# The seventh pair's transpose: by a DMA in its own unit, or by TensorE in the next

## The chip, the cores and the metric

The kernel runs on one core of one Trainium2 chip. The metric is the device time of one execution in microseconds (us), and of several runs the median. All times below are us, counted from the first instruction of the profiled execution, unless marked ns.

## What is computed

Softmax attention with an extra term in the denominator, over 8 batches of 12 heads (sequence 448, head dimension 64), and then a two-layer block with the Mish activation over all 3584 rows:

```python
scores = scale * np.matmul(q, k.transpose(0, 1, 3, 2))        # 8 x 12 x 448 x 448
m = np.max(scores, axis=-1, keepdims=True)
e = np.exp(scores - m)
attn = e / (np.sum(e, axis=-1, keepdims=True) + np.exp(-m) + 1e-09)
x = rows of matmul(attn, v)                                   # 3584 x 768
h = x @ w_in                                                  # 3584 x 2048
out = (h * np.tanh(softplus(h))) @ w_out                      # 3584 x 768, float32
```

## The kernel before

**Pairs, steps and units.** Two heads make a pair: 6 pairs a batch, 48 in all, counted from 0, so that the seventh is pair 6 (`HEAD`). A pair has 4 steps. A step is one or two score tiles (`scores`, TensorE, L264 to L281), their negated row maximum (`negm`, VectorE, L285), and one exponential per tile (`exps`, ScalarE, L298), which also gives the row sums and writes `en` (queries on partitions). Three PSUM tiles (`sc`) let TensorE run three steps ahead of ScalarE, and step n+3's scores wait until step n's exponentials have read their tile. The first six pairs run in a loop of their own. After that three pairs form a unit: units 2 to 15 have attention work, 12 steps each (numbered n = 0 to 11; "steps" below are these), and each unit ends in eight blocks of the first matmul with Mish (`mm1_mish`, L438 and L444). From unit 4 on, pieces of the second matmul (`mm2_part`, L485) are spread over the steps as well. The first matmul of a batch is spread over two units, one batch behind the attention: units 2 and 3 do that of pairs 0 to 5.

**Turning a pair.** The product with v (`av_pair`, L407) wants keys on partitions, so `en` must be transposed to `eT`. `normalise` does that with one DMA transpose on the SyncE (SP) queue (L370; 28 blocks of 128 x 128). `turn_on_pe` does it in four parts j: seven TensorE transposes into one PSUM bank (L381) and one copy to `eT` (L385), mostly on VectorE. Which pairs go which way is in `BY_PE`: pair 5 is turned on TensorE in steps 1 to 4 of unit 2, pair 6 in unit 3 (two parts at step 0, two at steps 2 and 3), pair 7 in steps 4 to 7 of unit 3. Pair 8 goes by DMA, issued at the end of unit 2. `eT` has three buffers; a new pair's transpose waits until the buffer's last reader, an `av_pair`, is done.

**Dividing.** Pairs 0 to 11 are divided after the product with v: `spread_rden` (L341, 16 small matmuls) spreads the reciprocals (in two bf16 parts `hl`, written by GpSimd at L322 and L323) over a PSUM bank, a copy brings it to SBUF as `rb` (L350), and the product's evacuation multiplies by it (`xT`, L419, VectorE). In unit 2 the copy of `rb` is on ScalarE, in units 3 and 4 on VectorE. `RDEN_AT` and `AV_AT` list at which step a pair's spread and product stand: in unit 3 at steps 7, 9, 10 and 8, 10, 11 for pairs 6, 7, 8.

**What sets the order.** There is no scheduler: each engine runs its instructions in the order in which the code emits them. Evacuations are put on a list (`late`) and emitted at the next step, right after its exponentials (`flush_late`). Two PSUM banks (`mo`) go round among the turns, spreads, products and the blocks of both large matmuls; each user waits until the bank's last evacuation is done. SP issues, in order: loads of q, k, v (L125, three per pair, three pairs ahead or more), the DMA transposes, and output rows. The casts of loaded pairs (L166 to L168) and the loads of weight pieces (L152) are on GpSimd, in one order too; `W_AT` says at which step a piece is loaded.

The first lines to look at are these two from the unit loop, which tell that an evacuation follows the next step's exponentials on its engine:

```python
            exps(idx)
            flush_late()
```

Of the kernel before, what the change touches and what calls it, by code (L numbers as in the profile page):

```python
# [15 lines left out]
UNIT_PAIRS = 3  # L16
# [3 lines left out]
def kernel(  # L20
# [9 lines left out]
    nc = tc.nc  # L30
# [5 lines left out]
    NT = 4  # L36
# [5 lines left out]
    UNITS_PER_B = HP // UNIT_PAIRS  # L42
# [6 lines left out]
    STEPS = 4  # L49
# [46 lines left out]
    LATE_DIV = 2 * HP  # L96
# [230 lines left out]
    def spread_rden(p, copy=None):  # L327

        own = mo_take()
        r = own[:, :]  # L330
        hl = att[p]["hl"]
        half = SP_ * NT - 3 * 128
        for at in range(4):
            for x in range(2):
                for h in range(2):
                    if at < 3:
                        rows, c, q0 = slice(0, 128), at + 4 * h, 128 * at + half * h
                    else:
                        rows, c, q0 = slice(half * h, half * h + half), 3, 3 * 128 * (1 - h)
                    n = rows.stop - rows.start  # L340
                    nc.tensor.matmul(  # L341
                        r[h * D : (h + 1) * D, q0 : q0 + n],
                        lhsT=hl[rows, x, c : c + 1].to_broadcast([n, D]),
                        rhs=ident[rows, rows],
                        start=(x == 0), stop=(x == 1),
                    )

        def evac():
            rb[p] = rb_pool.tile([128, S], FP32, tag="rb", name="rb")
            (copy or nc.scalar.copy)(rb[p], r[:, 0:S])  # L350
            mo_free.append(own)

        if copy is None:
            spread_copy[p] = evac
        else:
            late.append(evac)
# [18 lines left out]
    def turn_on_pe(p, j, act=False):  # L375

        st = att[p]
        own = mo_take()
        ps = own[:, :].bitcast(BF16).rearrange("c (i q) -> c i q", q=128)
        for i in range(NTILE):  # L380
            nc.tensor.transpose(ps[0:SP_, i, :], st["en"][:, j, i, 0:SP_], ident)  # L381
        copy = nc.scalar.copy if act else nc.vector.tensor_copy

        def evac():
            copy(  # L385
                out=st["eT"][0:SP_, j, :].rearrange("c (i q) -> c i q", q=128),
                in_=ps[0:SP_, 0:NTILE, :],
            )
            mo_free.append(own)

        late.append(evac)
# [134 lines left out]
    LOAD_AT = (0, 3, 6)  # L526
    HEAD = HP

    BY_PE = {HEAD - 1: 1, HEAD: 0, HEAD + 1: STEPS}
    AV_AT = {0: {6: 3, 8: 4, 10: 5}, 1: {8: 6, 10: 7, 11: 8}}  # L530
    RDEN_AT = {0: {5: 3, 7: 4, 9: 5}, 1: {7: 6, 9: 7, 10: 8}, 2: {3: 10, 7: 11}}
    TURN_BY_ACT = {(HEAD - 1, 3)}

    W_AT = ({1: 1, 5: 1, 9: 1}, {1: 1, 5: 1, 7: 1, 9: 1, 11: 1}, {1: 1, 3: 1, 5: 1, 7: 1})
# [14 lines left out]
    for p in range(HEAD):  # L549
        for s in range(STEPS):  # L550
# [23 lines left out]
            if s == 3:  # L574
                if p >= 3:
                    av_pair(p - 3, hold=True)
                if p + 5 < 10:
                    load_pair(p + 5)
                normalise(p, dma=p not in BY_PE)
    denominators(HEAD - 1)  # L580
# [3 lines left out]
    for u in range(UNITS_PER_B, N_UNITS + 2 * UNITS_PER_B):  # L584
        attn = u < N_UNITS
        filler = deque()
        for part in plan.get(u, []):
            filler.extend(mm2_part(*part))
        total, done, acc = sum(w for _, w in filler), 0, 0.0
        p0 = u * UNIT_PAIRS  # L590
        if attn and u >= first_mm2:
            av_with.update({p0 + i: p0 + i - UNIT_PAIRS for i in range(UNIT_PAIRS)})
        end = min((u + 1) * UNIT_PAIRS, N_PAIRS) * STEPS

        for n in range(steps):
            pi, s = divmod(n, STEPS)
            p, idx = p0 + pi, p0 * STEPS + n
            late_tp = u == UNITS_PER_B and n == STEPS
            if late_tp:
                transpose_pair(p0 + 2)  # L600
            exps(idx)
            if late_tp:
                evac_qk(p0 + 2)
            if u == UNITS_PER_B + 1 and n == 0:
                for j in range(2):
                    turn_on_pe(HEAD, j)
            flush_late()
            acc += weight[n]
            want = int(total * acc / sum(weight) + 1e-6)
            while done < want:  # L610
                fn, w = filler.popleft()
                fn()
                done += w
            scores_ahead(end)
            if n in LOAD_AT:
                load_pair(p0 + LOAD_AT.index(n) + LEAD)
                cast_pair(p0 + LOAD_AT.index(n) + LEAD - 1)
            spread = RDEN_AT.get(u - UNITS_PER_B, {})
            if n in spread:
                spread_rden(spread[n], copy=None if u == UNITS_PER_B else nc.vector.tensor_copy)  # L620
            early = AV_AT.get(u - UNITS_PER_B)
            if early is not None:
                if n in early:
                    av_pair(early[n])
                for pe, n0 in BY_PE.items():
                    first = 2 if pe == HEAD else 0
                    if pe // UNIT_PAIRS == u - 1 and n0 + first <= n < n0 + NT:
                        turn_on_pe(pe, n - n0, act=(pe, n - n0) in TURN_BY_ACT)
            elif s == (2 if pi else 0) and N_PAIRS <= p < N_PAIRS + UNIT_PAIRS:
                av_pair(p - UNIT_PAIRS)  # L630
            if u - UNITS_PER_B < len(W_AT):
                load_w(W_AT[u - UNITS_PER_B].get(n, 0))
        assert done == total

        moe = u < N_UNITS + UNITS_PER_B
        b, w = (u - UNITS_PER_B) // UNITS_PER_B, u % UNITS_PER_B
        nxt = p0 + UNIT_PAIRS
        todo = sorted(range(p0, nxt), key=lambda p: p in BY_PE)
        for f in range(FF_U):
            if moe:  # L640
                mm1_mish(b, w * FF_U + f)
            if u == UNITS_PER_B and f in (2, 6) or u == UNITS_PER_B + 1 and f == 1:
                load_w(1)
            if not attn:
                continue
            if f == 0:
                denominators(p0, UNIT_PAIRS)
                for p in todo if p0 < LATE_DIV else todo[:1]:
                    normalise(p, dma=p not in BY_PE)
            if f == 5 and u == UNITS_PER_B + 1:  # L650
                spread_rden(p0, copy=nc.scalar.copy)
            if f == 4:
                scores_ahead(min(nxt * STEPS + 1, N_PAIRS * STEPS))
            if f in (1, 3, 5):
                transpose_pair(nxt + f // 2, bank=f // 2 % 2)
                evac_qk(nxt + f // 2)
            if f >= FF_U - 2:
                scores_ahead(min(nxt * STEPS + f - FF_U + 4, N_PAIRS * STEPS))
            if f in (3, FF_U - 1) and p0 >= LATE_DIV:
                p = todo[1 + f // (FF_U - 1)]  # L660
                normalise(p, dma=p not in BY_PE)
    flush_late()
# [31 lines left out]
```

## Time and profile before

| what | value |
|---|---|
| three runs, us | 489.28, 492.48, 492.93 |
| median, us | 492.48 |
| profiled execution, us | 488.69 |
| its span, first to last instruction, us | 486.9 |
| mean granted TensorE clock | 0.987 |
| instructions | 9223 |
| the first six pairs | 0 to 45 |
| unit 2: steps, then its eight blocks | 45.0 to 61.3, to 72.6 |
| unit 3: steps, then its eight blocks | 72.6 to 91.6, to 103.7 |
| unit 4: steps, then its eight blocks | 103.7 to 120.5, to 131.9 |
| a later unit (5): steps, then blocks | 131.9 to 146.9, to 158.5 |
| DMA transpose on SP, issue time, us | 4.0 least, 4.2 median, 9.6 most |
| DMA transpose, issue to landing, us | 6.1 least, 6.6 median, 11.7 most |

How to read it: the profiled execution took 488.69 us, of which 486.9 lie between its first and last instruction. "Busy" of TensorE includes waiting inside a pipelined matmul. The three executions that were timed lie within 3.65 us of each other. PE is TensorE, PEld its weight loads, DVE VectorE, ACT ScalarE, POOL GpSimd, SPq the SyncE queue. In the table by stage each engine has its busy time and, in brackets, its number of instructions, then the granted clock (1.00 is full), the share of time in which the core's 16 DMA engines were busy (a transfer that straddles the edge of a stage counts whole, so it can pass 1), and GB/s.

### The profile page before, as it was taken

To read this page: it belongs to the slowest core of one execution; us is meant where nothing else is said; L and a number is where in the kernel's file an instruction comes from. 1 tells how busy PE (TensorE), PEld (TensorE's weight loads), DVE (VectorE), ACT (ScalarE), POOL (GpSimd) and SP (SyncE) were. 2 spreads that over 40 slices of the span, in tenths; PEclk is the share of its full clock that TensorE was granted. 3 is DMA by queue.
4 is the path that set the end of the run, shared out by engine and by line. 5 is a ranking of instruction groups with operands and counts; after the bars stand their busy time and mean duration, and the time that the engine had idled before them with its cause. 6 is when DMAs were issued, how large, how long until landed. Compare 5 with 4: busy or idle time off the path is not lost.

```text
span 486.9 us, 9223 instructions
## 1 busy us (share of the span) xinstructions
PE 453.3 (93%) x3219; PEld 258.4 (53%) x3219; DVE 359.4 (74%) x713; ACT 345.4 (71%) x905; POOL 103.4 (21%) x184
## 2 busy tenths in 40 slices
PE   4676896898999999999999999999999999999996
PEld 2344454554655565555555555555555555556563
DVE  4889738758889898889899888889898978520011
ACT  5998859677687887879687868788797968412300
POOL 4534535206013030403012120404040200000000
PEclk9999798999999999999999999999999999999999
DMA  8999999999998979799999998998979886761122
GB/s 233 221 235 206 265 197 241 145 185 246 143 220 224 204 195 197 230 194 258 164 247 174 221 209 190 223 199 223 199 236 164 210 152 142 146 146 31 36 59 72
DMA packets 204975, 91.08 MB, mean 187 GB/s; under 512 B 161792, under 2 KB 201472, under 8 KB 204928
## 3 DMA queue, kind: packets, MB, share of 16 engines
q1 hardware_dynamic: 197440, 84.20, 79.5%
q0 software_dynamic: 7488, 6.29, 9.0%
q8 instruction: 25, 0.41, 0.4%
q14 instruction: 22, 0.18, 0.1%
HBM read 45.61 MB, written 11.01 MB: 116 GB/s over the span
## 4 chain that ended last, share of the span: by engine, by line
PE 75%; ACT 11%; DVE 8%; DMA 2%; issue 2%; SPq 1%; POOL 0%; DVEq 0%; ACTq 0%
PE mo L438 26%; PE mo L485 24%; ACT en L298 9%; PE sc L264 7%; DVE negm L285 6%; PE sc L407 5%; PE sc L438 4%; PE sc L186 3%; PE mo L407 2%; DMA k_f<-in_k_dram 1%; PE mo L341 1%; PE sc L270 1%; DMA v_f<-in_v_dram 1%; SPq L125 1%; DVE eT L385 1%
## 5 line engine op out<-in xcount | busy, mean ns | idle before, releaser
L298 ACT ACTIVATE en<-sc,negm 128x448 bf16<-128x448 f32 x336 | 208.4, 641 | 22.6 <-DVE negm L285 20.7
L285 DVE TENSOR_REDUCE negm<-sc 128x2 f32<-128x896 f32 x192 | 183.0, 971 | 44.8 <-PE sc L264 28.2
L485 PE MATMUL mo<-w_out_sb,gT 128*128 128x384 bf16 (+1 forms) x1024 | 166.7, 306 | 0.0
L438 PE MATMUL mo<-xT,w_in_sb 128*128 128x448 bf16 x672 | 141.9, 353 | 0.5 <-DVE xT L417 0.3
L485 PEld LDWEIGHTS <-gT 128*128 128x128 bf16 x1024 | 96.3, 98 | 55.4 <-issue 1.3
L444 ACT ACTIVATE gT<-mo 128x448 bf16<-128x448 f32 x112 | 59.6, 543 | 83.0 <-PE mo L438 82.7
L438 PEld LDWEIGHTS <-w_in_sb 128*128 128x128 bf16 x768 | 72.7, 98 | 63.6 <-issue 3.3
L166 POOL CAST q_bf<-q_f 112x512 bf16<-112x512 f32 x47 | 29.3, 623 | 230.8 <-DMA q_f<-in_q_dram 208.0
L362 DVE TENSOR_SCALAR en<-en,rden 128x448 bf16<-128x448 bf16 x252 | 73.6, 365 | 0.8
L264 PE MATMUL sc<-kT,qd 128*128 128x448 bf16 x252 | 71.6, 354 | 0.0
L298 ACT ACTIVATION_READ_ACCUMULATOR en<-sc,negm 128x1 f32 x336 | 71.1, 212 | 0.0
L472 DVE COPY o_sb<-mo 128x384 f32<-128x384 f32 (+1 forms) x64 | 32.1, 501 | 48.3 <-PE mo L485 48.1
L264 PEld LDWEIGHTS <-qd 128*128 128x128 bf16 x252 | 24.6, 97 | 28.8 <-issue 12.9
L407 PE MATMUL sc<-eT,v_bf 112*64 112x448 bf16 x288 | 34.1, 357 | 2.1 <-ACT en L298 1.6
L223 DVE TENSOR_SCALAR qd<-sc 64x448 bf16<-64x448 bf16 x72 | 27.7, 385 | 7.5 <-PE sc L186 6.6
L407 PEld LDWEIGHTS <-v_bf 112*64 112x64 bf16 x384 | 20.9, 111 | 22.3 <-issue 15.6
L168 POOL CAST v_bf<-v_f 112x512 bf16<-112x512 f32 x48 | 29.9, 624 | 12.2 <-DMA v_f<-in_v_dram 11.5
L167 POOL CAST k_bf<-k_f 112x512 bf16<-112x512 f32 x47 | 29.1, 619 | 9.1 <-DMA k_f<-in_k_dram 8.0
L270 PE MATMUL sc<-kT,qd 64*128 64x448 bf16 x36 | 15.8, 457 | 7.7 <-ACT en L298 7.2
L186 PEld LDWEIGHTS <-q_bf 112*128 112x128 bf16 x192 | 14.3, 103 | 15.4 <-DVE q_bf L166 4.2
L231 ACT COPY kT<-sc 128x448 bf16<-128x448 bf16 x39 | 20.8, 534 | 0.6 <-PE sc L186 0.6
L438 PE MATMUL sc<-xT,w_in_sb 128*128 128x448 bf16 x96 | 20.8, 353 | 0.0
(53 smaller groups left out, 279.2 us busy)
## 6 DMA issues: line engine op xcount, KB each, us to landing
q_f<-in_q_dram SPq DMA_DIRECT2D x48, 224.0 KB, 5.3
k_f<-in_k_dram SPq DMA_DIRECT2D x48, 224.0 KB, 5.4
v_f<-in_v_dram SPq DMA_DIRECT2D x48, 224.0 KB, 5.5
w_in_sb<-in_moe_w_in_dram POOLq DMA_DIRECT2D x12, 256.0 KB, 7.3
w_out_sb<-in_moe_w_out_dram POOLq DMA_DIRECT2D x8, 384.0 KB, 7.4
out_dram<-o_sb SPq DMA_DIRECT2D x7, 336.0 KB, 3.5
out_dram<-o_sb SPq DMA_DIRECT2D x8, 288.0 KB, 5.0
out_dram<-o_sb SPq DMA_DIRECT2D x8, 240.0 KB, 3.5
```

The source lines that it names most:

```text
L166: cast_q(out=q_bf, in_=q_f.rearrange(by_t, t=NT))
L167: cast_k(out=k_bf, in_=k_f.rearrange(by_t, t=NT))
L168: nc.gpsimd.tensor_copy(out=v_bf, in_=v_f)
L264: nc.tensor.matmul(sc[:, bk, 0:S], lhsT=qT[:, i].rearrange("d h r -> d (h r)"), rhs=kT, start=True, stop=True,)
L285: nc.vector.tensor_reduce(out=negm, in_=sc[:, 0 : len(cols), 0:S], axis=AX.X, op=ALU.max, negate=True)
L298: e = nc.scalar.activation(out=st["en"][:, :, c, 0:SP_], in_=sc[:, bk, 0:S].rearrange("q (j c) -> q j c", j=NT), func=AF.Exp, bias=st["neg ...
L362: nc.vector.tensor_scalar(out=en[:, :, i, 0:SP_], in0=en[:, :, i, 0:SP_], scalar1=st["rden"][:, i : i + 1], scalar2=None, op0=ALU.mult,)
L407: nc.tensor.matmul(av[h * 64 : (h + 1) * 64, 0:S], lhsT=v_bf[:, h, j * D : (j + 1) * D], rhs=e_h, start=(j == 0), stop=(j == NT - 1),)
L438: nc.tensor.matmul(h_ps[:, 0:S], lhsT=w_in_sb[:, dm, ff * 128 : (ff + 1) * 128], rhs=xT[b][:, dm, :], start=(dm == 0), stop=(dm == DM_T - 1),)
L444: nc.scalar.activation(out=gT[:, ff, b % 2 * S : b % 2 * S + S], in_=h_ps[:, 0:S], func=AF.Mish)
L472: nc.vector.tensor_copy(out=o_sb[:, cols], in_=st["o"][:, 0:n_cols])
L485: nc.tensor.matmul(st["o"][:, 0:n_cols], lhsT=gT[:, ff, i * 128 : (i + 1) * 128], rhs=w_out_sb[:, ff, cols], start=(ff == 0), stop=(ff == ...
```

## The change

Pair 6 leaves `BY_PE`. Its DMA transpose is issued in unit 2 at step 7, behind the product of pair 3 at step 6, from whose buffer of `eT` it takes over. Its 28 transposes, 28 weight loads and four copies in unit 3 are gone. In unit 3 the spread and product of pair 6 move from steps 7 and 8 to steps 0 and 1, the turn of pair 7 from steps 4 to 7 to steps 2 to 5, the product of pair 7 stays at step 8 and its spread moves from 9 to 7, and the spread and product of pair 8 move from 10 and 11 to 9 and 10. The five copies of `rb` at L350 in units 3 and 4 (pairs 6, 7, 8 and 10, 11) go from VectorE to ScalarE.

```diff
-    BY_PE = {HEAD - 1: 1, HEAD: 0, HEAD + 1: STEPS}
-    AV_AT = {0: {6: 3, 8: 4, 10: 5}, 1: {8: 6, 10: 7, 11: 8}}
-    RDEN_AT = {0: {5: 3, 7: 4, 9: 5}, 1: {7: 6, 9: 7, 10: 8}, 2: {3: 10, 7: 11}}
+    BY_PE = {HEAD - 1: 1, HEAD + 1: 2}
+    AV_AT = {0: {6: 3, 8: 4, 10: 5}, 1: {1: 6, 8: 7, 10: 8}}
+    RDEN_AT = {0: {5: 3, 7: 4, 9: 5}, 1: {0: 6, 7: 7, 9: 8}, 2: {3: 10, 7: 11}}
...
-            if u == UNITS_PER_B + 1 and n == 0:
-                for j in range(2):
-                    turn_on_pe(HEAD, j)
             flush_late()
...
             if n in spread:
-                spread_rden(spread[n], copy=None if u == UNITS_PER_B else nc.vector.tensor_copy)
+                spread_rden(spread[n], copy=None if u == UNITS_PER_B else nc.scalar.copy)
...
                 for pe, n0 in BY_PE.items():
-                    first = 2 if pe == HEAD else 0
-                    if pe // UNIT_PAIRS == u - 1 and n0 + first <= n < n0 + NT:
+                    if pe // UNIT_PAIRS == u - 1 and n0 <= n < n0 + NT:
                         turn_on_pe(pe, n - n0, act=(pe, n - n0) in TURN_BY_ACT)
...
+            if u == UNITS_PER_B and n == 7:
+                normalise(p0)
...
-                for p in todo if p0 < LATE_DIV else todo[:1]:
+                for p in [p for p in todo if p != HEAD] if p0 < LATE_DIV else todo[:1]:
                     normalise(p, dma=p not in BY_PE)
```

## The prediction

> **What bounds the kernel now.** I read the page first, then busy times by stage, then the chain of work that ended last in the stages that the change touches, then the timelines of PE, DVE, ACT and SP there.
>
> ```profile
> span 486.9 us, 9223 instructions
> PE 453.3 (93%) x3219; PEld 258.4 (53%) x3219; DVE 359.4 (74%) x713; ACT 345.4 (71%) x905; POOL 103.4 (21%) x184
> PEclk9999798999999999999999999999999999999999
> DMA  8999999999998979799999998998979886761122
> ```
>
> PE is busy 93%, but two slices, the fifth and the seventh, have a lower clock: units 2 and 3. DMA is busy nearly everywhere.
>
> ```profile
> core 0: us, PE busy (x) PEld busy (x) DVE busy (x) ACT busy (x) POOL busy (x), PEclk, DMA share, GB/s
> 61.30:72.60 11.30, 11.30 (x78) 5.89 (x77) 4.34 (x8) 6.35 (x12) 4.25 (x8) 1.00 1.20 193
> 72.60:91.60 19.00, 13.16 (x149) 8.99 (x148) 16.12 (x23) 16.77 (x46) 6.46 (x10) 0.91 1.01 199
> 103.70:120.50 16.80, 14.10 (x120) 8.01 (x119) 11.73 (x16) 14.38 (x42) 7.38 (x12) 1.00 1.15 245
> 131.90:146.90 15.00, 15.00 (x105) 8.47 (x103) 12.69 (x22) 13.64 (x39) 1.84 (x3) 1.00 0.98 227
> ```
>
> From 131.9 on PE has no idle time in this stage: whatever is saved before moves all that follows, and reaches the end. In unit 3's steps (72.6 to 91.6) PE is idle 5.8 of 19 us, and DVE and ACT are busy 16.1 and 16.8. The chain there:
>
> ```profile
> 80.29 1.08 DVE negm L285
> 81.37 0.19 DVE eT L385
> ...
> 88.61 0.61 DVE xT L419
> 89.27 0.70 PE mo L341 x16
> 89.97 1.67 PE mo L407 x16
> 91.64 2.38 PE mo L438 x12
> ```
>
> DVE alternates row maxima with copies of `eT`, and at the end PE does the last spread and two products after the last exponentials, before the unit's first block at 91.64. SP:
>
> ```profile
> 60.74 5.53 SPq L370 DMA_TRANSPOSE eT<-en  x1
> 66.36 0.55 SPq L125 DMA_DIRECT2D q_f<-in_q_dram  x1
> 88.64 18.91 SPq L370 DMA_TRANSPOSE eT<-en  x3
> 107.64 0.53 SPq L125 DMA_DIRECT2D q_f<-in_q_dram  x1
> ```
>
> Pair 8's transpose, loads of pairs 13 to 15 behind it, then transposes of 9 to 11 that begin when pair 6's product (ends 88.6) frees a buffer.
>
> **The change, part by part: unit 3.** Durations are starts to next starts in the timelines: a row maximum 1.00 (two tiles) or 0.53, a copy of `eT`, of `rb` on DVE, or an `xT` 0.53, an exponential 0.61, `rb` on ACT 0.43 (0.54 busy, next start 0.43 later at 58.33), a turn on PE 0.5, a spread 0.65, a product 0.88, two scores 0.3.
>
> Removed from DVE: four `eT` copies (2.1) and three `rb` copies (1.6), 3.7 of its 16.1. Removed from PE: 28 transposes with weight loads, four turns of 0.5, or 1.0 where the clock is half. Added to ACT: 3 x 0.43 = 1.3. ACT then has 21 x 0.61 + 1.3 = 14.1 from 74.43 on and could at best end at 88.5 (now 89.27, with 1.3 of waits for DVE). So the exponentials cannot gain much. What gains is the tail: now spread 8 and products 7 and 8 stand after the last step; afterwards product 8 stands at step 10.
>
> I follow the four engines through the new order with these durations. Exponentials 0 and 1 end at 75.66 and 76.88 as now; scores 3 start at 75.82, then spread 6, scores 4, ACT copies `rb` 6 at 77.3 and does step 2 from 77.75 to 78.97. DVE: maximum 4 to 78.85, `xT` 6 to 79.55, maximum 5 to 80.55, then `eT`, maximum 6 to 82.08, `eT`, maximum 7 to 83.13, `eT`, maximum 8 to 84.66, `eT`, maximum 9 to 86.2. ACT: step 8 from 84.75 to 86.0 (now 84.00 to 85.23: DVE's row up to here still has four copies, and `xT` 6 is new), `rb` 7 to 86.43, step 9 to 87.66, step 10 to 88.9, `rb` 8 to 89.33, step 11 to 89.94. PE: scores 11 at 86.05, product 7 to 87.3, spread 8 to 87.95, product 8 at 88.35 to 89.2; the unit's first block needs the bank that `rb` 8 frees at 89.33, so it starts at 89.4 instead of 91.6. Exponentials end 0.7 later, yet this is hidden: table load to 91.45, first Mish to 92.0, and the fourth block, the first that needs its bank, starts at 93.2. **Unit 3: -2.2.**
>
> **The clock.** The trace gives the granted clock in stretches of 3.4 us:
>
> ```profile
> 71.60:75.00 3.40, 2.15 (x21) 1.34 (x20) 2.96 (x4) 2.40 (x4) 0.68 (x2) 1.00 1.13 288
> 75.00:78.40 3.40, 0.86 (x6) 0.38 (x5) 1.60 (x3) 3.40 (x13) 3.21 (x6) 1.00 1.12 276
> 78.40:81.80 3.40, 3.40 (x24) 2.20 (x23) 3.27 (x5) 3.30 (x11) 2.57 (x4) 0.52 1.14 197
> ```
>
> A stretch with PE busy 0.86 is followed by one at half clock; so are 1.47 (44.3 on) and 1.82 (51.1 on), while 1.95 (85.3 on) and 2.15 are not. Without the first two turns (0.99) the stretch from 71.6 has 1.16, so I let 75.0 to 78.4 run at half clock (spread 6 in 0.9, two scores in 0.55) and the next at full: this is in the -2.2. At full clock throughout it is -2.4. If the half clock fell on 85.3 to 88.7, scores 11, product 7 and spread 8 would end 1.1 later and the first block would start near 90.1: -1.5. The Trainium skill, "TensorE: Matmul & The Clock Gate", Part 4, says that a transpose does not count as PE work for the clock gate. By it, removing transposes leaves the clock as it was, and the sum would be about -2.4. The trace speaks against it: without transposes the stretch from 51.1 has 1.27 and is followed by half clock, that from 71.6 has 1.16 and is not.
>
> **Unit 2 and SP.** One DMA transpose is added. It waits for product 3 (ends 56.0 to 56.8) and the loads before it on SP (last issue 56.01), so it issues at about 56.9. Its price on SP is 4.0 to 9.6, in landing 6.1 to 11.7; in this saturated stretch its neighbours took 7.65 and 5.53, and 11.6 and 11.2, so I take 7.5 and 11.7: landed by 68.6, needed at 77.8. Behind it: pair 8's transpose from 60.74 to about 64.4, landed by 76 to 78, needed at 88.35; loads 13 to 15 from 66.4 to about 70, so casts of 13 and 14 on GpSimd from 74.0 to about 78, needed by transposes on PE from 94 on; then the last piece of `w_in` (76.24, now about 80, landed by 91), needed by the fifth block at 94.4; three pieces of `w_out` (78.7, now about 83). No compute engine waits: cost 0, cover 9, 10, 16 and 3 us. Transpose 9 no longer waits for product 6 at 88.6 (it goes near 79), so transposes 10 and 11 and the loads of 16 to 18, now from 107.64, come about 7 to 10 earlier; nothing on PE waits for these loads, so gain 0.
>
> **Unit 4.** Two `rb` copies go from DVE to ACT. Pair 10's delays steps 5 to 7 by 0.43, but step 8 waits for a maximum at 116.09 anyway. Pair 11's is emitted between steps 8 and 9 and waits for spread 11, which ends at 118.2 because its bank is freed by an output copy at 117.5: ACT, free at 117.3, stands until 118.2 and then copies, 1.4 for steps 9 and 10. Step 11 waits for DVE until 120.81 now; it would start at 121.2, so the first Mish comes at 123.35 instead of 122.96, done by 123.8, before the fourth block at 124.5 needs its bank. Cost 0, cover 0.7; without that cover at most the 0.4. It cannot gain: DVE's maxima 7 to 11 there wait for PE.
>
> **Sum.** -2.2 + 0 + 0 = -2.2 against the profiled execution of 488.69 (486.9 and 1.8 around it): 486.5. That run lies 3.8 under the median of the runs shown, 492.48, so I forecast 490.3.
>
> **Rivals.** (1) No change. What ends unit 3 is ACT, which gets 1.3 more work: its end moves from 89.27 to 89.94. For this, the first Mish must pace the blocks; against, it has 1.2 us of cover by my row. With the half clock in the tail as well, 0 to -1: 492.
>
> (2) Larger gain. DVE catches up early (the maximum of step 8 at 83.7 instead of 84.66), ACT runs nearly without waits to 88.5, the first block starts at 88.0, and unit 4 gains from an emptier DMA: -3.6 to -5, 488.5. Against it, `xT` 6 now lies in front of the copies.
>
> (3) Slower: the fourth piece of `w_out`. GpSimd issues it behind unit 3's `hl` at 93.35, and with 10.8 to landing it is there at 104.15; its first use is the 13th matmul from 103.72, at 105.7, only 1.5 later. Afterwards it is issued at about 91.3 for a use at 103.5, and transposes 10 and 11 and now also the loads of 16 to 18 share the engines. Nothing hides this: PE runs in order. From a landing over 12.2 it costs, over 14.4 the kernel is slower than before; at 16.2 (half more than now) PE waits 4.0, net +1.8: 494.3; at twice, +7.2: 499.7.
>
> (4) The transposed pair 6 comes late for product 6 at 77.8 and PE stands. It decides from a landing above 20.9 after issue, above 23.1 for a slower kernel; the longest of the 45 landings is 11.7. At three times that, 35.1, PE waits 14.2: 504.5. The Trainium skill, "VectorE: DVE Perf Modes", Rules for kernel authors, prefers TensorE for 128 x 128 transposes and lists 1309 ns for one by DMA: an estimate of 36.7 us for 28 of them, or about 506. The trace disagrees: 28 blocks land in 6.1 to 11.7.
>
> **How the numbers follow.** The forecast has 0.60, (1) 0.18, (2) 0.08, (3) 0.12, (4) 0.02. The likeliest gives 490.3. Its own bounds are -1.5 to -3.6, and the run scatter (489.28 to 492.93) adds about 1.5 on each side. The range must leave out no more than 2 in 10: it takes in (1) and most of (2), and the mild half of (3): 487.4 to 494.2. One per cent is 4.9 us, about what a measurement of this kernel can tell from no change. Faster by over that (under 487.6) needs most of (2): 0.07. Slower by over that (over 497.4) needs the heavy half of (3), or (4): 0.05. Within 1%: 0.88.
>
> **What would show it.** In the changed profile: 28 fewer transposes at L381 and four fewer copies at L385; a DMA transpose on SP at about 57, landed before 69, and no wait of PE's L407 for it; unit 3's first block at 89.4, with the last exponential about 0.7 later than now; a PE clock near half in 75 to 78.4 and not in the tail; no idle PE before the second matmul's 13th piece near 103.5; in unit 4 a wait of ACT's L350 of about 0.9. If the first block starts at 91 or later, or PE waits near 103, the forecast is wrong.

## The result, and the profile after

The changed kernel takes 496.78 us in the median of 17 runs (493.49 to 500.11), the kernel before 492.42 in 17 runs (489.22 to 496.51): the ratio is 1.010, with a 95% interval of 1.0068 to 1.0133. Here and below a median counts all executions, while a ratio leaves out those over 1.5% above the fastest of their kernel. The forecast was 490.3 with a range of 487.4 to 494.2, and the time lies above it. The profiled execution after took 494.53, 5.84 more than that of before (488.69). The page after begins so:

```profile
span 492.8 us, 9163 instructions
...
PE 453.8 (92%) x3191; PEld 256.0 (52%) x3191; DVE 353.0 (72%) x704; ACT 347.3 (70%) x910; POOL 103.3 (21%) x184
...
PEclk9998998989999999999999999999999999999999
DMA  8999999999999979999998989898998886770122
```

The change did what it says: 28 matmuls fewer, nine DVE instructions fewer, five on ACT more; DVE is busy 6.4 us less, and PE does not profit. The busy times by stage, with the columns as in the table of before: unit 2's blocks, unit 3's steps, unit 3's blocks, unit 4's steps. Below them stands the row of before for unit 3's blocks.

```profile
core 0: us, PE busy (x) PEld busy (x) DVE busy (x) ACT busy (x) POOL busy (x), PEclk, DMA share, GB/s
...
62.50:73.80 11.30, 11.26 (x78) 5.89 (x77) 4.37 (x8) 6.36 (x11) 4.49 (x9) 1.00 1.40 141
73.80:90.90 17.10, 11.46 (x121) 6.60 (x120) 12.19 (x17) 15.97 (x46) 6.46 (x10) 0.90 1.17 240
90.90:108.70 17.80, 13.83 (x95) 7.58 (x95) 7.01 (x17) 7.70 (x16) 3.67 (x8) 0.90 1.36 145
108.70:126.40 17.70, 14.42 (x120) 7.84 (x119) 10.69 (x14) 14.48 (x41) 4.54 (x8) 1.00 1.19 220
```

```profile
91.60:103.70 12.10, 12.10 (x96) 6.86 (x95) 6.96 (x17) 5.80 (x12) 3.62 (x7) 1.00 1.31 157
```

Against before: unit 2's blocks begin at 62.5 and not at 61.3 (+1.2; the first six pairs, which the change does not touch, ended later in this execution), unit 3's steps take 17.1 and not 19.0 (-1.9), unit 3's blocks 17.8 and not 12.1 (+5.7), unit 4's steps 17.7 and not 16.8 (+0.9); from there to the end of the span 366.4 in both. The sum is +5.9, the difference of the spans. So the saving came nearly as forecast, and it was lost in the 17.8 us of unit 3's blocks. PE's timeline tells to what:

```profile
90.87 2.43 PE L438 MATMUL mo<-xT,w_in_sb 128*128 128x448 bf16 x12 [0.15 <-ACT rb L350]
...
96.20 0.92 PE L438 MATMUL mo<-xT,w_in_sb 128*128 128x448 bf16 x4
...
101.10 0.55 PE L438 MATMUL mo<-xT,w_in_sb 128*128 128x448 bf16 x2 [3.97 <-DMA w_in_sb<-in_moe_w_in_dram]
...
112.25 0.48 PE L485 MATMUL mo<-w_out_sb,gT 128*128 128x384 bf16 x2 [1.47 <-DMA w_out_sb<-in_moe_w_out_dram]
```

In the middle of the fifth block PE stands 3.97 for the last piece of `w_in`, and in unit 4 another 1.47 for the fourth piece of `w_out`. Why the pieces are late begins on SP and is handed on by GpSimd. First SP; then GpSimd after (cast of pair 13, last piece of `w_in`, fourth piece of `w_out`); then the same cast and the same piece of `w_in` before:

```profile
58.82 20.52 SPq L370 DMA_TRANSPOSE eT<-en  x2
79.43 0.53 SPq L125 DMA_DIRECT2D q_f<-in_q_dram  x1
...
84.99 32.27 SPq L370 DMA_TRANSPOSE eT<-en  x3
117.36 0.53 SPq L125 DMA_DIRECT2D q_f<-in_q_dram  x1
```

```profile
83.13 0.61 POOL L166 CAST q_bf<-q_f 112x512 bf16<-112x512 f32 x1 [15.03 <-DMA q_f<-in_q_dram]
...
85.74 0.71 POOL L152 DMA_DIRECT2D w_in_sb<-in_moe_w_in_dram  x1
...
92.74 0.79 POOL L152 DMA_DIRECT2D w_out_sb<-in_moe_w_out_dram  x1
```

```profile
73.99 0.61 POOL L166 CAST q_bf<-q_f 112x512 bf16<-112x512 f32 x1 [7.12 <-DMA q_f<-in_q_dram]
...
76.24 0.71 POOL L152 DMA_DIRECT2D w_in_sb<-in_moe_w_in_dram  x1
```

The added transpose and pair 8's take 20.5 of SP together (5.5 for pair 8's alone before). The loads of pairs 13 to 15 behind them go out at 79.4 instead of 66.4, so GpSimd stands 15.0 at the first cast of pair 13 (7.1 before), and the last piece of `w_in` behind that cast is issued at 85.7 instead of 76.2; it lands in 15.3 instead of 5.3. At 85.0 transposes 9 to 11 start, and take 32.3 of SP instead of 18.9. Issue to landing in 55 to 125, before and then after (last column, median us):

```profile
w_out_sb<-in_moe_w_out_dram POOLq DMA_DIRECT2D x8, 384.0 KB, 7.4
...
w_in_sb<-in_moe_w_in_dram POOLq DMA_DIRECT2D x6, 256.0 KB, 6.3
...
eT<-en SPq DMA_TRANSPOSE x5, 11.2
```

```profile
w_out_sb<-in_moe_w_out_dram POOLq DMA_DIRECT2D x7, 384.0 KB, 16.6
...
w_in_sb<-in_moe_w_in_dram POOLq DMA_DIRECT2D x6, 256.0 KB, 11.3
eT<-en SPq DMA_TRANSPOSE x5, 16.6
```

Weight pieces and transposes land late together. The chain of work that ended last runs through one of them, for 35.4% of the stretch from 60 to 115:

```profile
92.52 0.21 POOL hl L323
92.74 19.46 DMA w_out_sb<-in_moe_w_out_dram
...
112.25 0.48 PE mo L485 x2
```

The fourth piece of `w_out` was issued at 92.74, right behind `hl`, for which GpSimd had stood idle, and so not held up by the late piece of `w_in`. So with this landing PE would have stood at that place until 112.2 even with `w_in` in time: the wait of 3.97 is the larger one, but the chain passes it by. Before, the fourth piece landed in 10.7.

The wait for `w_in` is paid a second time by the clock. Stretches of 3.4 us after (PEclk is the third column from the right):

```profile
98.80:102.20 3.40, 1.10 (x6) 0.60 (x7) 0.14 (x1) 0.51 (x1) 0.00 (x0) 1.00 1.28 188
102.20:105.60 3.40, 3.40 (x31) 2.05 (x29) 1.43 (x3) 0.57 (x2) 0.00 (x0) 0.53 1.28 194
```

PE is busy 1.10 of the stretch with the wait, and the next one, in which PE is busy throughout, runs at 0.53: 0.47 x 3.4 = 1.6 us. With the wait that is 5.6 of the 5.7 that unit 3's blocks lost.

### The profile page after: what moved, and what is told of

Same layout as the page of the kernel before. It is cut to its first block, busy times and chain, and to the rows that moved or that the text cites. A ratio compares the mean times of both kernels' runs of the same rounds, so it can differ in the third digit from the quotient of the medians.

```text
span 492.8 us, 9163 instructions
## 1 busy us (share of the span) xinstructions
PE 453.8 (92%) x3191; PEld 256.0 (52%) x3191; DVE 353.0 (72%) x704; ACT 347.3 (70%) x910; POOL 103.3 (21%) x184
## 4 chain that ended last, share of the span: by engine, by line
PE 72%; ACT 11%; DVE 8%; DMA 5%; issue 2%; SPq 0%; POOL 0%; DVEq 0%; ACTq 0%
PE mo L438 24%; PE mo L485 24%; ACT en L298 10%; PE sc L264 7%; DVE negm L285 6%; PE sc L407 6%; DMA w_out_sb<-in_moe_w_out_dram 4%; PE sc L438 3%; PE sc L186 3%; PE mo L407 2%; DMA k_f<-in_k_dram 1%; DVE eT L385 1%; PE mo L341 1%; PE sc L270 1%; ACT rb L350 1%
## 5 line engine op out<-in xcount | busy, mean ns | idle before, releaser
L362 DVE TENSOR_SCALAR en<-en,rden 128x448 bf16<-128x448 bf16 x252 | 72.6, 361 | 0.8
L264 PE MATMUL sc<-kT,qd 128*128 128x448 bf16 x252 | 71.5, 354 | 0.1
L168 POOL CAST v_bf<-v_f 112x512 bf16<-112x512 f32 x48 | 29.7, 618 | 12.6 <-DMA v_f<-in_v_dram 12.1
```

Of the source, the lines that this page charges most:

```text
L168: nc.gpsimd.tensor_copy(out=v_bf, in_=v_f)
L264: nc.tensor.matmul(sc[:, bk, 0:S], lhsT=qT[:, i].rearrange("d h r -> d (h r)"), rhs=kT, start=True, stop=True,)
L362: nc.vector.tensor_scalar(out=en[:, :, i, 0:SP_], in0=en[:, :, i, 0:SP_], scalar1=st["rden"][:, i : i + 1], scalar2=None, op0=ALU.mult,)
```

## The experiments

Theory V (volume): between 58 and 118 us the core's sixteen DMA engines are the bound; loads, weight pieces and four transposes are just in time, and with a fifth something that PE needs is late, whichever it is. Rival O (order): only the place of the new transpose ahead of the loads on SP counts. Rival X (crossing): transposes and weight pieces slow each other to more than the sum of their times when they are in flight together. In some of the expectations Q is the hand-over just shown (the transpose on SP holds up loads, these the casts, these the weight pieces), C a cost of the new order of the engines' work, and A a guess that each expectation states for itself. "Ratio" is against the kernel before in runs on the same chip, with its 95% interval.

One execution of each run was profiled, and its time is not always near the median: that of e4 is the shortest of its twelve, those of e8, e9, e17 and e19 are the longest of theirs. A wait that is read below is the wait of that one execution.

### Which part of the change is it: e2, e3, e13

e2: the kernel before, with only a transfer added, at the place of the change.

```diff
+            if u == UNITS_PER_B and n == 7:
+                nc.sync.dma_start_transpose(
+                    out=gT[:, 12:16, :].rearrange("c f (i q) -> c (f i) q", q=128),
+                    in_=att[HEAD]["en"][:, :].rearrange("q j i c -> q (j i c)"),
+                )
```

> The kernel before, with pair 6 turned on TensorE as it was, plus one DMA transpose of pair 6 at step 7 of unit 2 whose output nobody reads (it goes to a part of gT that is not yet in use). Theories Q and V: the transfer alone costs what the change lost plus what its compute gained, 4.4 + 2.2 = 6.6, so about 499, with waits of TensorE for w_in and w_out. Rival C (the new order of the compute engines costs the time, and the transfer is hidden): 492.4, as before.

498.75 in the median, ratio 1.010 [1.0057, 1.0144]: the whole loss, without any change of the engines' work. PE stands 4.6 for `w_in` and 3.3 for `w_out`, at the same places as in the changed kernel:

```profile
102.49 0.79 PE L438 MATMUL mo<-xT,w_in_sb 128*128 128x448 bf16 x2 [4.61 <-DMA w_in_sb<-in_moe_w_in_dram]
...
113.36 0.81 PE L485 MATMUL mo<-w_out_sb,gT 128*128 128x384 bf16 x4 [1.52 <-DMA w_out_sb<-in_moe_w_out_dram]
...
115.95 0.48 PE L485 MATMUL mo<-w_out_sb,gT 128*128 128x384 bf16 x2 [1.77 <-DMA w_out_sb<-in_moe_w_out_dram]
```

e3: the kernel after without the new transpose (product 6 reads pair 5's turned copy).

```diff
-                normalise(p0)
+                att[p0]["eT"] = att[HEAD - 1]["eT"]
```

> The changed kernel without the DMA transpose of pair 6: the product of pair 6 reads the turned tile of pair 5 instead, so one transpose is left out and everything else is as in the changed kernel. Theories Q and V: no wait for w_in or w_out, and the gain of the new order alone shows, 492.4 - 2.2 = about 490.2. Rival C: 496 or more, as the changed kernel.

493.04, ratio 1.0002 [0.9964, 1.0039]. The loss is gone, but the saving does not show in the median, although unit 3's steps are 1.7 shorter in the profiled execution (494.21, of twelve from 486.98 to 495.5): PE still waits there. The waits of PE in 55 to 140 (total, times, longest):

```profile
PE mo L438 <- DMA w_in_sb<-in_moe_w_in_dram: 3.2, 1, 3.2
...
PE mo L485 <- DMA w_out_sb<-in_moe_w_out_dram: 1.2, 1, 1.2
```

In the old order transposes 9 to 11 began at 88.6; now they begin at 81.3, on top of the last weight pieces, and take 35.8 of SP. The last piece of `w_in` lands in 18.0 (5.3 before). But it was also issued at 83.2 (76.2 before), behind casts of which the first had waited 10.2 for its load before any of these transposes began. So e3 does not tell by itself whether the early start or four transposes as such cost the saving; e15 and e18 below take this up.

e13: the kernel before with the copies of `rb` of units 3 and 4 on ScalarE (`nc.scalar.copy` for `nc.vector.tensor_copy` in the call of `spread_rden`), nothing else.

> The kernel before with one part of the change alone: the five copies of rb in units 3 and 4 on ScalarE. No transfer and no order changes. VectorE has 1.6 less of its 16.1 in unit 3, ScalarE 1.3 more; the tail of spread 8 and products 7 and 8 stays, with the copies of rb behind the last exponentials on ScalarE: between -1.0 and +0.5 of the kernel before, under what can be measured. If it is slower by over 1, the copies are part of the loss and the transfer is not all of it.

492.75, ratio 0.9992 [0.9955, 1.0028]: this part costs nothing that can be measured and gains nothing.

### Does the late piece decide, or the order: e1, e9, e10, e11

e1: the kernel after, with the last piece of `w_in` ahead of the casts of pair 13 on GpSimd.

```diff
-    W_AT = ({1: 1, 5: 1, 9: 1}, {1: 1, 5: 1, 7: 1, 9: 1, 11: 1}, {1: 1, 3: 1, 5: 1, 7: 1})
+    W_AT = ({1: 1, 5: 1, 9: 1}, {1: 2, 7: 1, 9: 1, 11: 1}, {1: 1, 3: 1, 5: 1, 7: 1})
```

> The changed kernel, but the last piece of w_in is issued by GpSimd one step after unit 3 begins (step 1, next to the piece before it), ahead of the casts of pair 13 that wait for their load, instead of behind them (step 5). Theory Q (queue order: the added transpose holds up the loads of pairs 13 to 15 on SP, the casts that wait for them hold up the weight pieces behind them on GpSimd, and TensorE then waits 4.0 us for w_in): the piece is issued near 68 instead of 85.7, the wait of TensorE for w_in is gone, and the time falls by 4 to 5, to about 492. Theory V (volume: the 16 DMA engines have no room left between 58 and 118, so something else comes late instead): a piece still lands late or the wait shows up elsewhere, at w_out or at a product, and the time stays at 495.5 to 497.

491.9, ratio 0.9993 [0.996, 1.0025]. The wait for `w_in` is gone, the fourth piece of `w_out` lands in 13.4 (19.5 in the kernel after), and the loss is gone, but two other waits take the saving:

```profile
82.47 1.71 PE L407 MATMUL mo<-eT,v_bf 112*64 112x448 bf16 x8 [2.65 <-DMA eT<-en]
...
110.12 0.49 PE L485 MATMUL mo<-w_out_sb,gT 128*128 128x384 bf16 x2 [1.10 <-DMA w_out_sb<-in_moe_w_out_dram]
```

Three more orders were tried on top of e1. e9 also puts transpose 10 ahead of 9, away from the weight pieces; e10 issues all pieces of unit 2 at its steps 1 and 5 and none among its blocks; e11 moves spread and product 6 to steps 5 and 6, where its transpose cannot be late.

```diff
# e9: e1, and ahead of each unit's blocks
+        if u == UNITS_PER_B + 1:
+            todo = [p0 + 1, p0, p0 + 2]
# e10 (and no load_w(1) in the blocks of unit 2)
-    W_AT = ({1: 1, 5: 1, 9: 1}, {1: 1, 5: 1, 7: 1, 9: 1, 11: 1}, {1: 1, 3: 1, 5: 1, 7: 1})
+    W_AT = ({1: 3, 5: 2}, {1: 2, 7: 1, 9: 1, 11: 1}, {1: 1, 3: 1, 5: 1, 7: 1})
# e11: e1, and
-    BY_PE = {HEAD - 1: 1, HEAD + 1: 2}
+    BY_PE = {HEAD - 1: 1, HEAD + 1: 0}
-    AV_AT = {..., 1: {1: 6, 8: 7, 10: 8}}
+    AV_AT = {..., 1: {6: 6, 8: 7, 10: 8}}
-    RDEN_AT = {..., 1: {0: 6, 7: 7, 9: 8}, ...}
+    RDEN_AT = {..., 1: {5: 6, 7: 7, 9: 8}, ...}
```

> The changed kernel with both cures: the last piece of w_in ahead of the casts of pair 13, and transpose 10 ahead of transpose 9 in unit 3. With the first alone it took 491.9, and TensorE still waited 2.7 for the transposed pair 6 and 1.1 for w_out. Theory X: a little less than 491.9, 490 to 491.5, since the wait for w_out goes but that for pair 6 stays. Theory V: 491.9 or more.

> The changed kernel with the weight pieces that GpSimd issues around transposes 6 and 8 moved ahead of them: three pieces at step 1 and two at step 5 of unit 2 instead of one each at steps 1, 5, 9 and two among its blocks, and the last w_in piece ahead of the casts of pair 13. Theory A (the engines take packets of a transpose and of a weight piece in turn, one for one, so a transpose of 3584 short packets crawls as long as pieces are in flight, and with it everything behind it on SP): transposes 6 and 8 take about 10 on SP instead of 20.5, the loads of pair 13 issue near 70, and no wait for w_in or the turned pair 6 is left: 489 to 491.5. Theory V (volume alone): the same bytes must pass before 100, so the waits move and the time is 492 or more.

> The changed kernel with the last w_in piece ahead of the casts of pair 13 (491.9 with this alone, with a wait of 2.7 for the turned pair 6 at step 1 of unit 3), and with spread and product 6 at steps 5 and 6 instead of 0 and 1 (the turn of pair 7 at steps 0 to 3). Theory A: the late transpose 6 has five more steps, so the wait of 2.7 goes, and transpose 9, which waits for product 6, starts some 6 us later and meets fewer of the weight pieces: 489 to 490.5. Rival: the wait turns up at product 8 or at w_out instead: 491.5 to 493.

| run | median | ratio | PE waits for transfers in its profile, us |
|---|---|---|---|
| e9 | 496.06 | 1.0087 [1.0057, 1.0117] | `eT` 5.2 (product 6) and 3.9 (product 9), `w_out` 0.2 |
| e10 | 493.0 | 1.0007 [0.9974, 1.004] | `eT` 6.2 (product 6 for most of it), `w_out` 2.1 |
| e11 | 493.64 | 1.0041 [1.0009, 1.0073] | `w_out` 3.7 |

Every order takes one wait away and makes another. None is faster than before, and e1, with e10 hardly behind, is the best of them: with these five transposes the order settles whether the fifth costs 1% or nothing. In e10 transposes 6 and 8 took 22.9 on SP (20.5 after) and not the 10 expected; but four weight pieces still went out beside them, at 64.7 and 70.4, so the guess behind that number was not put to the test.

### Crossing or volume: e6, e4, e5, e8

e6 computes nothing of the reference, and it ran once. It runs three transposes, five `w_out` pieces and nine loads by themselves, then in pairs (beside transposes the loads are issued by ScalarE); each phase ends when DVE has read all that it brings.

> Transfers alone, in stages that wait for one another: three DMA transposes of 28 blocks; five pieces of w_out on GpSimd's queue; nine q, k, v loads; then transposes with pieces, loads with pieces, transposes with loads. It computes nothing of the reference and writes zeros. Theory X: transposes with pieces take clearly more than the sum of the two alone (three transposes alone about 16 to landing, five pieces alone about 8 to 10, together 30 to 40), while loads with pieces take about their sum. Theory V: every mix takes about the sum of its parts, at most 26 for transposes with pieces.

Alone: transposes 15.0 (one more every 4.2), pieces 13.0, loads 9.7. Transposes with pieces 25.4 (sum 28.0), loads with pieces 21.5 (22.7), transposes with loads 21.0 (24.7). No mix takes more than its sum, so X falls as far as this one run goes; but within a mix the transposes, which land at 6.4, 10.7 and 15.0 when alone, land at 10.6, 22.3 and 25.4. DVE reads them as they land, alone from 2.96 and mixed from 41.84 on:

```profile
9.41 0.16 DVE L53 TENSOR_TENSOR acc<-acc,eT 128x1 f32<-128x1 f32 x1 [6.36 <-DMA eT<-en]
13.71 0.16 DVE L53 TENSOR_TENSOR acc<-acc,eT 128x1 f32<-128x1 f32 x1 [4.14 <-DMA eT<-en]
17.93 0.16 DVE L53 TENSOR_TENSOR acc<-acc,eT 128x1 f32<-128x1 f32 x1 [4.06 <-DMA eT<-en]
...
52.46 0.16 DVE L53 TENSOR_TENSOR acc<-acc,eT 128x1 f32<-128x1 f32 x1 [10.23 <-DMA eT<-en]
64.11 0.16 DVE L53 TENSOR_TENSOR acc<-acc,eT 128x1 f32<-128x1 f32 x1 [11.49 <-DMA eT<-en]
67.24 0.16 DVE L53 TENSOR_TENSOR acc<-acc,eT 128x1 f32<-128x1 f32 x1 [2.97 <-DMA eT<-en]
```

The other three test the same on the kernel. e4: e3, with a plain copy of the same 0.92 MB (`nc.sync.dma_start` into `gT[:, 12:16, :]`) where the transpose was. e5: e3, with transpose 10 ahead of 9 (as in e9). e8: the kernel after with pair 6 turned on PE in unit 2's steps 8 to 11, and transpose 10 ahead of 9.

```diff
# e8 (and transpose 10 ahead of 9, as in e9)
-                normalise(p0)
+                normalise(p0, dma=False)
+            if u == UNITS_PER_B and n >= 8:
+                turn_on_pe(p0, n - 8)
```

> As the kernel without the transpose of pair 6, but in its place on SP stands a plain DMA copy of the same 0.92 MB of en to a part of gT that nobody reads. If any transfer of that size at that place delays the rest (order on SP, bytes), the time is 495 to 497. If it is the transpose as such that keeps the DMA engines for long (its short packets), the copy costs at most 1 and the time is 490 to 491.5.

> As the kernel without the transpose of pair 6 (which reads the turned tile of pair 5 and gained nothing, though its unit 3 was 1.7 us shorter), but in unit 3 the transpose of pair 10 stands ahead of that of pair 9 on SP, so that no transpose starts near 81 any more; the first waits for product 7, near 87. Theory X (a DMA transpose and weight loads that are in flight together hold each other up, and the early product 6 let transpose 9 start in the middle of the last weight loads): the three transposes take nearer 19 than 36 on SP, TensorE waits less than 1 for w_in, and the 2.2 of the new order show: about 490. Theory V (only the volume counts, and it is unchanged): 492 to 493 as without this.

> The changed kernel with pair 6 turned in its own unit by TensorE (steps 8 to 11 of unit 2, copies on VectorE) instead of by a DMA transpose, and with transpose 10 ahead of transpose 9 in unit 3. Theory X: no extra transfer and no early transpose, so unit 3's 2.2 are kept; unit 2 gets four turns (2 of TensorE, 2.1 of VectorE, which have 3.5 and 4 idle there) and loses at most 1.5: 489.8 to 491.5. Theory V: the same transfers as before, hence the same as X here; a time of 493 or more would speak against both, and mean that the new order itself costs.

e4: 492.54, ratio 0.9995 [0.9958, 1.0033], between the two expected ranges; the time is that of e3. So the same bytes at the same place cost nothing that can be measured if they are not transposed. That does not mean that nothing behind the copy was held up. In e4's profile, of its shortest execution (486.83), the copy took 0.56 on SP and landed in 8.3, yet pair 8's transpose behind it took 14.5 on SP (6.6 in e3) and the loads of pair 13 went out at 74.6 (68.8); the last piece of `w_in`, issued at 80.7, landed in 11.1, in time. The pages of e3, of the kernel after and of e4 differ in the packets that they count:

```profile
DMA packets 204975, 91.08 MB, mean 185 GB/s; under 512 B 161792, under 2 KB 201472, under 8 KB 204928
DMA packets 208591, 92.00 MB, mean 187 GB/s; under 512 B 165408, under 2 KB 205088, under 8 KB 208544
DMA packets 205120, 92.00 MB, mean 190 GB/s; under 512 B 161809, under 2 KB 201489, under 8 KB 205073
```

The 0.92 MB go in 3616 packets more with the transpose, all under 512 bytes, and in 145 more with the copy. That the number of packets is the reason was not tried.

e5: 497.25 in the median, but its times fall in two groups (three from 488.7 to 489.9, nine from 494.9 to 501.3); the ratio, 0.9975 [0.9925, 1.0025], rests on four of the twelve and settles nothing. e8: 492.04, ratio 1.0011 [0.9983, 1.0039], a little over the range that both theories gave (489.8 to 491.5): in its profile unit 2's steps are some 4 longer by the turn, where at most 1.5 was expected, and product 9 waits 3.9 for its late transpose.

### How many transposes: e15, e16, e17

e15: e3 with pair 8's transpose left out as well (product 8 reads pair 7's copy). e16: the kernel before without pair 8's. e17: the kernel after with one transfer more, the lines of e2's diff behind `normalise(p0)`.

```diff
# e15 and e16
-                    normalise(p, dma=p not in BY_PE)
+                    normalise(p, dma=p not in BY_PE and p != HEAD + 2)
+                if p0 == HEAD:
+                    att[HEAD + 2]["eT"] = att[HEAD + 1]["eT"]
```

> The kernel after without the DMA transposes of pairs 6 and 8 (product 6 reads pair 5's turned copy, product 8 that of pair 7), so three transposes (9 to 11) are left between 57 and 118 us where the kernel before has four and the kernel after five. Theory V (the sixteen DMA engines are the bound in that stretch, and the saving of 1.9 us in unit 3 is given back as a wait for whatever transfer is last): with 8.4 us of transfers less than after, and 4.2 less than before, no wait of PE for w_in or w_out over 0.7, the saving stays: 488.5 to 490.5, ratio to before 0.993 to 0.996. Rival O (only the order on SP and GpSimd counts, so removing more bytes without moving a load ahead does nothing more than removing pair 6's transpose did): 492 to 494, ratio about 1.000, the wait for w_in still over 2.

> The kernel before without the DMA transpose of pair 8 (product 8 reads pair 7's turned copy): three transposes in the stretch instead of four, no change of the compute engines' work. Theory V: the kernel before has little transfer left to gain from, since its waits there are short (about 1): 490.5 to 492, ratio 0.996 to 1.000. Rival O: the loads of 13 to 15 go some 5 us earlier, and that alone decides: the same 490.5 to 492; told apart from V only together with the other two runs. If it is over 494, both fall.

> The kernel after with one more DMA transpose, of pair 6's tile into a part of gT that nobody reads then, right behind the one that the change adds: six transposes in the stretch. Theory V: 4.2 us more of transfers on engines that are already the bound, all of it paid, or more since the first transposes in a mix are the ones that are held up: 501 to 504, ratio to before 1.018 to 1.025. Rival O (the price is one place on SP, already paid): 497 to 499, ratio 1.010 to 1.014. Rival X (each further transpose costs more than the last): over 506.

Median and ratio by the number of transposes that go by DMA in 57 to 118:

| transposes | engines' work as before | engines' work as after |
|---|---|---|
| 3 | e16: 491.09, 1.0001 [0.9984, 1.0019] | e15: 489.23, 0.9949 [0.9924, 0.9975] |
| 4 | before: 1 | e3: 493.04, 1.0002 [0.9964, 1.0039] |
| 5 | e2: 498.75, 1.010 [1.0057, 1.0144] | after: 496.78, 1.010 [1.0068, 1.0133] |
| 6 | | e17: 499.82, 1.0173 [1.0129, 1.0218] |

With three transposes there is no wait of PE for a transfer, and the new work is 1.86 faster than the old (489.23 against 491.09): most of the forecast's -2.2, seen at last in the time. The kernel before gains nothing from a transpose less, since PE waits for no transfer there either. So in the order of before the fourth transpose is free, and the fifth costs 1.0%; in the order of after the fourth costs 0.5%, the fifth 1.0% and the sixth 0.7%, where 4.2 us would be 0.9%. The landing of the fourth piece of `w_out` goes with it: in the profiles of the new work it is 8.4 with three transposes (e15), 18.4 with four (e3), 19.5 with five, 19.4 with six (e17). e17 came out between what V (501 to 504) and O (497 to 499) expected. Its waits have moved from `w_in` to `w_out`:

```profile
PE mo L485 <- DMA w_out_sb<-in_moe_w_out_dram: 6.6, 4, 3.0
...
PE mo L407 <- DMA eT<-en: 1.6, 1, 1.6
...
PE mo L438 <- DMA w_in_sb<-in_moe_w_in_dram: 1.0, 1, 1.0
```

e15 has a flaw: without pair 8's transpose the loads of pairs 13 to 15 went out at 59.2 already, so volume and order changed together.

### Volume without order, order without volume: e18, e19

e18 is e15 with SP held back by 1 KB that waits for the fourth Mish of unit 2. e19 is the kernel after with pair 8's transpose behind the loads of pair 13.

```diff
# e18: e15, and behind mm1_mish in the block loop
+            if u == UNITS_PER_B and f == 3:
+                nc.sync.dma_start(out=gT[0:2, 12, 0:256], in_=gT[0:2, 3, 0:256])
# e19: pair 8 left out of the loop at f == 0, and behind load_pair and cast_pair
+            if u == UNITS_PER_B + 1 and n == 0:
+                normalise(HEAD + 2)
```

> The kernel of the run before with three transposes (after, without the DMA transposes of pairs 6 and 8; products 6 and 8 read other pairs' turned copies), and in the place of pair 8's transpose a transfer of 1 KB into an unread part of gT that waits for the fourth Mish of unit 2: SP stands there until about 69, so the loads of pairs 13 to 15 go out no earlier than with four transposes (68.76), and not at 59 as they did with three. Theory V (what was too much is the transposes' share of the sixteen engines): the casts of pair 13 find their data by about 76 all the same, no wait of PE for w_in over 1, 489 to 491, ratio to before 0.993 to 0.998. Rival O (the place of the loads in SP's order): the casts of pair 13 are as late as with four transposes (79.2), the last piece of w_in lands near 101, PE waits over 2 for it, 492 to 494.5, ratio 0.999 to 1.005.

> The kernel after, all five transposes as they are, but pair 8's DMA transpose is issued behind the loads of pair 13 (step 0 of unit 3) and not ahead of them, so that its place in the order of SP is the only thing that changes. Rival O: loads of 13 at about 69, casts near 76, the last piece of w_in issued at 78, no wait of PE for it, and the saving of 1.9 us shows: 489 to 491, ratio 0.993 to 0.998. Theory V: the same amount still has to pass, so another transfer is late, pair 8's turned copy for product 8 at 88 or the fourth piece of w_out; PE waits 2 or more in all and the saving does not show: 491.5 to 495, ratio 0.999 to 1.007.

e18: 489.16, ratio 0.9931 [0.9902, 0.996]. SP and GpSimd:

```profile
70.46 0.75 SPq L643 DMA_DIRECT2D gT<-gT  x1
71.31 0.33 SPq L125 DMA_DIRECT2D q_f<-in_q_dram  x1
...
82.79 25.48 SPq L370 DMA_TRANSPOSE eT<-en  x3
```

```profile
75.81 0.61 POOL L166 CAST q_bf<-q_f 112x512 bf16<-112x512 f32 x1 [5.30 <-DMA q_f<-in_q_dram]
...
77.81 0.71 POOL L152 DMA_DIRECT2D w_in_sb<-in_moe_w_in_dram  x1
```

The loads go out at 71.3, 2.5 later than in e3 (68.8), and are there in 4.5, so that the cast starts at 75.8, 3.4 earlier than in e3 (79.2). The last piece of `w_in` is issued at 77.8 and lands in 5.0. PE waits for no transfer, and the saving shows. So it is pair 8's transpose itself that cost e3 its saving, and not the place of the loads behind it; the strict form of O falls. Transposes 9 to 11 begin as early here (82.8; 81.9 in e15) as in e3 (81.3), so an early start alone does not cost the saving either: here the last piece of `w_in` had just landed when they began. e19: 491.37, ratio 0.9978 [0.9943, 1.0014], between the two expectations. Its profiled execution, the longest of its twelve, has no wait for `w_in`, but 3.5 for pair 6's `eT` and 3.0 for `w_out`.

### A version that keeps the turn on TensorE: e14

The kernel before with the order of e1 and the copies of e13.

> The kernel before with the copies of rb on ScalarE and the last w_in piece ahead of the casts of pair 13. Theory A: in the kernel before this piece was issued at 76.2 and needed near 96, so little depends on it; only those runs that lay 4 to 6 above the median should become fewer: median 490.5 to 491.5. Theory V: no difference.

491.03, ratio 0.9968 [0.9939, 0.9997]. That lies in the range of Theory A. It is the fastest of the versions that compute the whole, by less than the runs can tell from e1 or e19, and it has one DMA transpose less than the changed kernel.

## Why the prediction was wrong

**Unit 3, -2.2: right, and a little large.** The steps took 17.1 for 19.0 (-1.9), the first block came at 90.87, 17.1 after the unit's start (forecast 16.8, from 72.6 to 89.4), and it waited for the copy of `rb` 8 as forecast. e15 against e16 gives 1.86 in the time. The half clock fell one stretch later than I let it (0.54 in 78.3 to 81.7, behind a stretch with 1.03 of PE busy), where it was before: the unit began 1.2 later, so the stretch from 71.5 still had 2.57 of PE and not 1.16. What it cost there was not measured apart, and it does not decide between the two readings of the clock in the prediction, since the stretch before it has little PE work by either.

**The `rb` copies and unit 4, 0: right** (e13: 0.9992). In unit 4 the copy of `rb` 11 waits 0.93 for its spread, as forecast (0.9); what unit 4's steps lost, 0.9, stands beside a wait of 1.47 for `w_out`.

**Unit 2 and SP: this step failed.** "No compute engine waits: cost 0, cover 9, 10, 16 and 3 us." It took the landing of the new transpose from its neighbours (11.7) and moved the traffic behind it by about 4 without making any of it slower. In fact the transpose landed in 19.6, and pair 8's behind it took 11.1 on SP and not 5.5. The loads of pair 13 were issued at 79.4 (forecast about 70), the last `w_in` piece at 85.7 (forecast about 80), and it landed at about 101 (forecast 91) for a use at 97: the cover of 3 was overdrawn by 4.0. The fourth piece of `w_out`, which the sum put at nothing and left to rival (3), landed in 19.5 (10.7 before). The covers were taken one by one, each against the landing times of before, on DMA engines that the page shows busy nine tenths or more in every slice of that stretch; e2 shows that one transpose added there makes others late, with the engines' work as before.

**"Transpose 9 no longer waits ... so gain 0": failed too.** Transposes 10 and 11 and the loads of pairs 16 to 18 were to come 7 to 10 earlier. Transpose 9 did start earlier, at 85.0 (88.6 before; forecast near 79), but the three then took 32.3 of SP (18.9), and those loads went out at 117.4, 9.7 later than before. That this start costs time by itself is not shown: e5, which takes it away, settles nothing, and e15 and e18, which have it, keep the saving.

**Rival (3) was the nearest.** Its piece, the fourth of `w_out`, was issued at 92.74 and landed in 19.46, and the chain of work passes through it. By its own rule (the kernel is slower above a landing of 14.4) that is 19.46 - 14.4 = 5.1 over before, about what was measured (4.4 between the medians). It came with `w_in` in front, which no rival named: the wait of 3.97 and the half clock behind it had made the use later, so that only 1.47 of waiting was left for this piece. That the two numbers lie so near is in part luck: one is of a single execution, the other of medians. The page's DMA line, nine tenths or more in every slice there, spoke for more than the 12% that this rival was given. Rival (4) did not come in the changed kernel, where the landing of 19.6 stayed under its 20.9; in e1, e9 and e10, where the weights were moved ahead, product 6 waited for it (2.7 to 5.6). The Trainium skill, "DMA: Bandwidth & Descriptors", "Issuing engines are not separate DMA queues", says that transfers from SP, ScalarE and GpSimd run on the same sixteen engines and interleave. e6 agrees: transposes from SP and pieces from GpSimd take 25.4 together, near the sum of 28.0. Read so, a free SP says nothing of free engines.

**What stays open.** Why the transposes are the ones that crawl in a mix, and the plain copy of e4 costs no time that can be measured, was not tried further than e4 and e6. How the loss of five transposes splits between volume and order depends on the order: e1 and e19 recover all of it, none of them the saving (e19's interval leaves room for a part). Why the executions of one kernel differ by as much as e3's do (486.98 to 495.5) is open too.

## What to carry to other kernels

Where the DMA line of a stage reads nine tenths, do not price an added transfer at nothing: take it as time of all engines (here 4.2 for a transpose, measured alone; the fifth and the sixth cost about that, though e1 and e19 got the fifth for nothing by order) and ask which of the transfers behind it has the least cover, on every queue. Follow the hand-over from SP to GpSimd and to PE: a late load held up a cast, the cast a weight piece, and the piece a matmul two hops away from the change. And a step that is freed early starts its own transfers early, into whatever is then in flight.

## What the runs showed of the hardware

- DMA transposes of 28 blocks, alone, land one every 4.2 (at 6.4, 10.7 and 15.0 in e6). In a mix with weight pieces the first two landed 11.7 apart in e6, and in the kernel one landed in 19.6.
- The Trainium skill, "Advanced Engine Details and Errata", "X-Bar Transpose (TRN2)", says that transposes by DMA are as fast as regular ones. Alone e6 agrees roughly: three transposes, 2.75 MB, in 15.0, nine loads, 2.06 MB, in 9.7. Beside other transfers the runs differ: the plain copy of e4 landed in 8.3 at the same place in the kernel, the transpose in 19.6.
- A wait of PE can cost again by the clock: 3.97 of waiting was followed by 3.4 at 0.53, 1.6 more.
